# Two of four chunks of the residual x in SBUF, the others in HBM, and the room given to exp outputs and shift buffers

## The chip, the cores and the metric

The kernel runs on one core of a Trainium2 chip. The core has five instruction queues that run beside each other and wait for one another through semaphores: PE (matrix products), ACT (functions such as exp), DVE (vector work), POOL (a second, smaller vector engine) and SP, which here issues the DMAs. Each queue runs its instructions in the order in which they were written down. SBUF is the memory on the core, with 128 partitions; PSUM holds the results of PE in 8 banks; HBM is the large memory, which only DMAs reach. The metric is the device time of one execution in microseconds (us), as the median of several runs.

## The reference

```python
x = A_x                                   # 1 x 2048 x 512, bf16
for layer in range(2):
    # attention, 32 heads of 16
    qkv = layernorm(x) @ wqkv
    p = softmax(q @ k.T * 0.25)           # 2048 x 2048 for each head
    x = x + (p @ v) @ wo
    # dense block
    h = gelu(layernorm(x) @ w1 + b1)      # 2048 x 1792
    x = x + h @ w2 + b2
return x
```

Both layers use the same weights. The norm has no scale or shift of its own.

## The kernel before

**Tiles.** The 2048 tokens are 16 tiles of 128, and four chunks of four tiles. Chunk 0 is tiles 0 to 3, and so on. The residual x lies in SBUF the whole time, as `T["X"]` (L449): 16 tiles of 512 numbers in each partition, 16 KB of bf16 a partition. The attention is worked off in passes (`passes`, L1034): one pass is one chunk of queries, two heads side by side in a tile, and a range of key tiles. Each pass has 64 tiles of scores of 128 x 512 (16 key tiles by four column groups), in sum 4096 over both layers; the first and last passes are cut differently.

**One tile of scores.** PE makes it from `kt` and `qp` (L1168). Its exp is made in one of two ways. On ACT, `exps` (L1503) takes two or three tiles of PSUM at a time (the banks of `SLOTS`, L20) into units of the ring `pt`. On DVE, `dfirst` (L1317) turns one tile from PSUM into 16-bit integers whose bits are nearly the exp, in a buffer of `du`; then `dchain` adds 32 to it (L1378) and 64 to both (L1380), so that four shifted copies stand there. PE multiplies those with V and with three scaled copies of V (`vc`, L1099), and the mean of the four is the better exp. So a DVE tile needs four products where an ACT tile needs one (both L1566, in `pvs`). Only four key tiles of 16 have scaled copies and may go to DVE (`KD`, L45), 512 tiles of scores a layer.

**Buffers.** `pt` has `PT_RING` = 19 units of 1 KB a partition, and borrows parts of K, Q and V when they are not in use (`setup_units`, L1417). `du` has `DU` = 9 tile slots of 4 KB a partition: four pairs, and one half buffer called `dh` (L469 to 473). A pair runs L1378 and L1380 once for two tiles, the half buffer once for one. In layer 1 a fifth pair is borrowed from K of layer 0 (L474, the groups named `kt` in the profile); `cap` (L1083) lists the sizes. A slot is bound when the score's product is issued (`join`, L1207) and free when the last of the four products is issued.

**The order.** Nothing is decided on the chip. When the program is built, `_Sched` (L213) runs the whole computation with costs written beside each operation, and appends each to its engine's list at the time when it would start; semaphore waits follow from what each operation reads and writes (`_Prog`, L81). Threads such as `scores`, `exps`, `pvs` and `post` are Python generators; they yield operations, take units from pools ("acq", "rel") and wait for tokens ("need", "give"). `attach` (L1249), `swap` (L1226) and `solo` (L1325) give a tile to DVE if a slot of `du`, a bank (7, 6, or the third of slot 0) and an eligible tile are to be had and DVE is not behind. `pvs` takes DVE tiles first while more than `PTLOW` = 5 units of `pt` are free, and else ACT tiles (L1550); its products become more urgent with fewer than `PTURG` = 6 free units or with no free `du` buffer (L1542). SP's DMAs are ordered by the same planner, one list for all.

**What uses x.** `loads` (L572) brings it in: chunk 0 in four tiles, chunks 1 to 3 in one DMA each (L578). Three layer norms per chunk follow, which the code calls phases: phase 0 before the projections of layer 0, phase 2 before those of layer 1, phases 1 and 3 before the dense blocks. A norm reads x twice: for statistics on DVE (L612), and for the normalized tile on POOL (L633; on DVE for chunk 0's first one and for the last piece), which a DMA transposes (L637). `wo` adds the attention's output to x (L816), `ytile` the dense block's (L956), both on DVE; in layer 1 `ytile` then writes the tile out (L961). Between these, each chunk of x is not touched for the length of several passes. `post` (L971) runs all of this for a chunk while the passes of the next chunk go on. Weights for it come through a ring of four buffers, one DMA each (`wload`, L858, the DMA in L860).

Of the kernel before, what the change touches and what calls it, by code (L numbers as in the profile page):

```python
# [12 lines left out]
D = 512  # L13
# [7 lines left out]
PVB = 5  # L21
MISC = (6, 7)
DBANK = (7,)
PT_RING = 19
LEND = (3, 2)
QP_RING = 3
W_RING = 4
W_MORE = 4
XLN_RING = 2
GP = 2  # L30

DU = 9
LNP = 7
SWAP = 0.5
ALONE = 3.5
# [392 lines left out]
def bass_interleave_layers__mha_block__dense_activation_gelu__prompt_kernel(  # L428
    nc: bass.Bass,
    A_x: bass.AP,  # L430
    A_wqkv: bass.AP,
    A_wo: bass.AP,
    B_x: bass.AP,
    B_w1: bass.AP,
    B_b1: bass.AP,
    B_w2: bass.AP,
    B_b2: bass.AP,
    out: bass.AP,
):
    S = A_x.shape[1]  # L440
    assert S % 512 == 0 and A_x.shape[2] == D
    NT = S // 128

    with ExitStack() as es:
        def sb(shape, dt, name):
            return es.enter_context(nc.sbuf_tensor(name, shape, dt))

        T = {}
        T["X"] = sb([128, NT, D], BF16, "x")  # L449
        wr = sb([128, W_RING, 1024], BF16, "wr")  # L450
        T["K"] = [sb([128, NDC, S], BF16, "kt%d" % l) for l in range(NL)]
        vf = [sb([128, NT * H * 17], BF16, "v%d" % l) for l in range(NL)]
        T["V"] = [v[:, :].rearrange("p (k h c) -> p k h c", k=NT, h=H) for v in vf]
        T["WR"] = [wr[:, i, :] for i in range(W_RING)]
        T["WR"] += [T["K"][0][:, i // 2, 1024 * (i % 2):1024 * (i % 2) + 1024] for i in range(W_MORE)]
        T["Q"] = sb([128, NDC, S], BF16, "q")
        T["QP"] = sb([128, QP_RING, 512], BF16, "qp")
        T["OTN"] = sb([128, NDC, 512], BF16, "otn")
        T["XF"] = sb([128, NDC, 512], BF16, "xf")
        T["XLN"] = sb([128, XLN_RING, D], BF16, "xln")  # L460
        T["G"] = sb([128, NFC, 512], BF16, "g")
        T["WQKV"] = T["G"][:, 0:12, :].rearrange("p (w c) d -> p w c d", w=3)
        pt = sb([128, PT_RING, 512], BF16, "pt")
# [24 lines left out]
        T["STATS"] = sb([128, NT, 6], F32, "stats")  # L488
        T["MV"] = sb([128, NT, 2], F32, "mv")
        T["VARR"] = sb([128, NT], F32, "varr")  # L490
        T["RSTD"] = sb([128, NT], F32, "rstd")
        T["NMR"] = sb([128, NT], F32, "nmr")
        PS = es.enter_context(nc.psum_tensor("ps", [128, 8 * 512], F32))

        sem_names = ["pe", "act", "dve", "pool", "dxt0", "dxt1", "dxt2", "dxt3", "dx1", "dx2", "dx3", "dwq", "dwk", "dwv", "db1", "db2"] + ["dw%d" % c for c in range(3)] + [
                     "dout"] + ["dwr%d" % i for i in range(W_RING + W_MORE)] + ["dtr%d" % i for i in range(XLN_RING)]
        sems = {n: es.enter_context(nc.semaphore("s_" + n)) for n in sem_names}
        P = _Prog(sems)
        hbm = dict(x=A_x.rearrange("b (n p) d -> p (b n) d", p=128), out=out.rearrange("b (n p) d -> p (b n) d", p=128),
                   wqkv=A_wqkv, wo=A_wo, w1=B_w1, b1=B_b1, w2=B_w2, b2=B_b2)  # L500
        _Plan(P, S, T, PS, hbm).run()

        with nc.Block() as block:
            @block.tensor
            def _(eng):
                P.emit("pe", eng)

            @block.scalar
            def _(eng):
                P.emit("act", eng)  # L510

            @block.vector
# [20 lines left out]
class _Plan:  # L533
# [38 lines left out]
    def loads(self):  # L572
        T, hbm = self.T, self.hbm

        def load(dst, src, sem, keys, cost):
            return _Op("sp", cost, lambda e: e.dma_start(dst, src), writes=keys, sem=sem, by=16, tail=2.0)

        def lx(c):  # L578
            return load(T["X"][:, 4 * c:4 * c + 4, :], hbm["x"][:, 4 * c:4 * c + 4, :], "dx%d" % c,
                        ["X.%d" % t for t in range(4 * c, 4 * c + 4)], 2.5)  # L580

        def lw(i, sem):
            return load(T["WQKV"][:, i, :, :], hbm["wqkv"][:, i * D:(i + 1) * D].rearrange("(c p) f -> p c f", p=128),
                        sem, ["W.%d" % i], 2.5)

        for t in range(4):
            yield load(T["X"][:, t, :], hbm["x"][:, t, :], "dxt%d" % t, ["X.%d" % t], 0.6)
        yield lw(1, "dwk")
        yield lw(0, "dwq")
        yield lw(2, "dwv")  # L590
        yield lx(1)
        yield lx(2)
        yield lx(3)
        yield load(T["B1c"][:], hbm["b1"].rearrange("(c p) -> c p", p=128), "db1", ["B1c"], 0.2)
        yield _Op("sp", 0.2, lambda e: e.dma_start(T["B2row"][0:1, :], hbm["b2"].rearrange("(o e) -> o e", o=1)),
                  reads=["B2zero"], writes=["B2row", "B2zero"], sem="db2", by=16, tail=2.0)
# [5 lines left out]
        yield ("rel", "misc", b)  # L602
        yield ("give", "loaded")

    def ln(self, tiles, dst, dkeys, prio, quick=False):

        T = self.T
# [1 line left out]
        sl = slice(c, c + n)  # L609
        for t in tiles:  # L610
            yield ("need", ("xready", t, self.phase[t // 4]))
            yield _Op("dve", 0.66, lambda e, t=t: e.bn_stats(T["STATS"][:, t, :], T["X"][:, t, :]),  # L612
                      reads=["X.%d" % t], writes=["ST.%d" % t])
            yield _Op("dve", 0.17, lambda e, t=t: e.bn_aggr(T["MV"][:, t, :], T["STATS"][:, t, :]),
                      reads=["ST.%d" % t], writes=["MV.%d" % t])
        mvk = ["MV.%d" % t for t in tiles]
# [11 lines left out]
    def ln_tile(self, c, t, dst, dkeys, quick):  # L628
# [2 lines left out]
        x = yield ("acq", "xln")  # L631
        eng, cost = ("dve", 0.4) if quick else ("pool", 1.0)
        yield _Op(eng, cost, lambda e: e.tensor_scalar(  # L633
            T["XLN"][:, x, :], T["X"][:, t, :], T["RSTD"][:, t:t + 1], T["NMR"][:, t:t + 1], op0=ALU.mult, op1=ALU.add),
            reads=["X.%d" % t, "RSTD.%d" % c, "NMR.%d" % c], writes=["XLN.%d" % x])
        if not quick:
            yield _Op("sp", 0.3, lambda e: e.dma_start(dst(t), T["XLN"][:, x, :], transpose=True),  # L637
                      reads=["XLN.%d" % x], writes=dkeys(t), sem="dtr%d" % x, by=16, tail=3.5)
# [158 lines left out]

    def wo(self, l, seg, t):
        T = self.T
        for gb in range(4):  # L800
            yield ("need", ("otn", l, seg, gb))
        us = []
# [10 lines left out]
                      writes=["B.%d" % b], prio=MID if h else FPRIO, mode="P")  # L813
        for j in range(2):
            yield from self.wdone((l, seg, "O", j), us[j])
        yield _Op("dve", DV, lambda e: e.tensor_tensor(out=T["X"][:, t, :], in0=T["X"][:, t, :], in1=pb, op=ALU.add),  # L816
                  reads=["B.%d" % b, "X.%d" % t], writes=["X.%d" % t])
        yield ("rel", "misc", b)
        yield ("give", ("xready", t, 2 * l + 1))

# [51 lines left out]
    def tiles(self, seg):  # L872
        return range(4 * seg[0] + seg[1] // 128, 4 * seg[0] + (seg[1] + seg[2]) // 128)
# [54 lines left out]
    def ytile(self, l, seg, t):  # L928
# [9 lines left out]
        for p in range(NFC // 2):  # L938
# [14 lines left out]
                      writes=["B.%d" % b], prio=MID if p else FPRIO, mode="P")  # L953
            if not tail or p == last:
                yield from self.wdone(piece, w)
        yield _Op("dve", DV, lambda e: e.tensor_tensor(out=T["X"][:, t, :], in0=T["X"][:, t, :], in1=pb, op=ALU.add),  # L956
                  reads=["B.%d" % b, "X.%d" % t], writes=["X.%d" % t])
        yield ("rel", "misc", b)
        yield ("give", ("xready", t, 2 * l + 2))
        if l == NL - 1:  # L960
            yield _Op("sp", 1.0, lambda e: e.dma_start(self.hbm["out"][:, t, :], T["X"][:, t, :]), reads=["X.%d" % t],  # L961
                      writes=["OUT.%d" % t], sem="dout", by=16, tail=2.0)

    def when(self, l, seg, part):
        return lambda: self.scored >= min(self.base[(l, seg)] + part * self.span[(l, seg)], self.total)
# [56 lines left out]
    def first(self, c):  # L1022
        T = self.T
        self.phase[c] = 0
        for t in range(4 * c, 4 * c + 4):
            yield ("give", ("xready", t, 0))
        tiles = range(4 * c, 4 * c + 4)
        for ts in (tiles,) if c else ([t] for t in tiles):
            yield ("spawn", self.ln(ts, lambda t: T["K"][1][:, :, t * 128:(t + 1) * 128], lambda t: ["XL.%d" % t], 5 + c, c == 0), 5 + c)
# [631 lines left out]
```

## Time and profile before

| what | value |
|---|---|
| median of 3 runs | 1567.77 us (1567.01 to 1567.84) |
| the profiled execution | 1563.99 us |
| its span, first to last instruction | 1562.1 us |
| ACT exps of `pt` (L1503) | 1248 instructions, 1336.7 us |
| scores on PE (L1168) | 4096 products |
| DVE tiles (L1317) into `du`, `dh`, `kt` | 748, 98, 88 |
| first DVE tile, last DVE tile | 65.1 us, 1524.2 us |
| DMA traffic | 96.84 MB |
| weight loads (L860) on SP, B weights | 256 of 256 KB, landing after 2.8 us |

How to read the profile: "busy" is the time in which an engine ran instructions, as a sum and as a share of the span. In a row of a group stand the line, the engine, what is written and read, and the count; behind the bar follow the busy time in us, the mean duration of one in ns, and the idle time just before these with what ended it. In a row of a window stand the window, its length, each engine's busy time and count, the clock granted to PE, the share of DMA and GB/s. In a row of a wait stand who waited for what, the total in us, how often, and the longest. The chain is followed back from the last instruction: at each step to what released it. In a row of DMAs stand the count, the size of one and the median us from issue to landing. The program's span up to some 70 us is the opening (chunk 0 alone, no DVE tiles), 70 to 780 is the rest of layer 0, 780 to 1530 layer 1, and the rest the ending.

### The profile page before, as it was taken

To read this page: it belongs to the slowest core of one execution; us is meant where nothing else is said; L and a number is where in the kernel's file an instruction comes from. 1 tells how busy PE (TensorE), PEld (TensorE's weight loads), DVE (VectorE), ACT (ScalarE), POOL (GpSimd) and SP (SyncE) were. 2 spreads that over 40 slices of the span, in tenths; PEclk is the share of its full clock that TensorE was granted. 3 is DMA by queue.
4 is the path that set the end of the run, shared out by engine and by line. 5 is a ranking of instruction groups with operands and counts; after the bars stand their busy time and mean duration, and the time that the engine had idled before them with its cause. 6 is when DMAs were issued, how large, how long until landed. Compare 5 with 4: busy or idle time off the path is not lost.

```text
span 1562.1 us, 42238 instructions
## 1 busy us (share of the span) xinstructions
PE 1443.7 (92%) x18537; PEld 432.7 (28%) x18537; DVE 1369.9 (88%) x2653; ACT 1523.5 (98%) x1412; POOL 210.5 (13%) x250
## 2 busy tenths in 40 slices
PE   8999889999999999999989999888998989999998
PEld 2222222222222222222222222222222222233344
DVE  5689999979898989978799798999999988898893
ACT  7999999999999999999999999999999999999995
POOL 5300001002020101102030021122002010010000
PEclk9999999999999999999999899999999999999999
DMA  5100001052113310133111331001151105313430
GB/s 143 22 1 1 2 15 35 29 163 55 42 42 116 99 46 26 40 120 102 36 35 42 118 94 42 2 1 35 56 166 52 35 15 161 98 36 96 150 83 29
DMA packets 141765, 96.84 MB, mean 62 GB/s; under 512 B 36877, under 2 KB 141582, under 8 KB 141582
## 3 DMA queue, kind: packets, MB, share of 16 engines
q1 hardware_dynamic: 141582, 94.14, 20.8%
q8 instruction: 146, 2.39, 0.6%
q14 instruction: 37, 0.30, 0.1%
HBM read 84.41 MB, written 2.10 MB: 55 GB/s over the span
## 4 chain that ended last, share of the span: by engine, by line
ACT 65%; PE 24%; DVE 10%; issue 1%; DMA 0%; POOL 0%; ACTq 0%; DVEq 0%
ACT pt L1503 56%; PE ps L543 9%; PE ps L1168 8%; PE ps L1566 6%; DVE du L1317 4%; ACT g L924 3%; ACT kt L1503 2%; ACT v L1503 2%; DVE du L1380 2%; ACT q L1503 1%; DVE du L1378 1%; ACT L924 1%; DVE dh L1317 1%; ACT L1503 0%; PE ps L1156 0%
## 5 line engine op out<-in xcount | busy, mean ns | idle before, releaser
L1503 ACT ACTIVATE pt<-ps 128x1024 bf16<-128x1024 f32 (+1 forms) x1248 | 1336.7, 1232 | 10.7 <-PE ps L1168 8.0
L1168 PE MATMUL ps<-qp,kt 32*128 32x512 bf16 x4096 | 557.8, 386 | 49.7 <-ACT pt L1503 35.0
L1317 DVE TENSOR_SCALAR du<-ps 128x512 uint16<-128x512 f32 x748 | 498.9, 682 | 78.7 <-PE ps L1168 76.3
L1566 PE MATMUL ps<-pt,v 128*17 128x512 bf16 (+1 forms) x3245 | 454.2, 360 | 25.1 <-ACT pt L1503 20.2
L1566 PE MATMUL ps<-du,vc 128*17 128x512 bf16 (+1 forms) x2502 | 353.7, 360 | 8.7 <-ACT pt L1503 5.6
L1168 PEld LDWEIGHTS ps<-qp,kt 32*128 32x128 bf16 x4096 | 143.5, 91 | 611.6 <-ACT pt L1503 409.1
L1380 DVE TENSOR_SCALAR du<-du 128x2048 uint16<-128x2048 uint16 x377 | 257.6, 687 | 2.7
L1116 POOL TENSOR_SCALAR qp<-q,mask 128x512 bf16<-128x512 bf16 (+1 forms) x91 | 80.9, 889 | 958.0 <-PE ps L1168 947.8
L543 PE MATMUL ps<-xf,wr 128*32 128x512 bf16 (+1 forms) x2400 | 168.5, 368 | 1.4 <-DVE g L903 0.7
L1566 PE MATMUL ps<-du,v 128*17 128x512 bf16 (+1 forms) x834 | 160.9, 361 | 6.8 <-DVE v L770 3.1
L1378 DVE TENSOR_SCALAR du<-du 128x1024 uint16<-128x1024 uint16 x377 | 156.4, 424 | 2.5
L1566 PEld LDWEIGHTS ps<-pt,v 128*17 128x17 bf16 x3245 | 111.0, 89 | 138.3 <-issue 64.2
L543 PE MATMUL ps<-wr,g 128*32 128x512 bf16 x1600 | 126.3, 391 | 4.9 <-ACT g L924 4.3
L1566 PEld LDWEIGHTS ps<-du,vc 128*17 128x17 bf16 x2502 | 90.2, 89 | 83.3 <-issue 43.0
L1566 PE MATMUL ps<-dh,vc 128*17 128x512 bf16 (+1 forms) x330 | 95.6, 358 | 0.0
L903 DVE TENSOR_SCALAR g<-ps,hb1t 128x512 bf16<-128x512 f32 (+1 forms) x112 | 79.3, 708 | 5.4 <-PE ps L543 5.0
L1317 DVE TENSOR_SCALAR dh<-ps 128x512 uint16<-128x512 f32 x98 | 66.7, 681 | 1.2 <-PE ps L1168 1.1
L543 PEld LDWEIGHTS ps<-xf,wr 128*32 128x32 bf16 x2400 | 48.1, 95 | 63.0 <-issue 41.0
L1317 DVE TENSOR_SCALAR kt<-ps 128x512 uint16<-128x512 f32 x88 | 60.1, 683 | 5.9 <-PE ps L1168 5.0
L1156 PE MATMUL ps<-vc 128*32 128x512 bf16 x576 | 55.5, 408 | 8.3 <-DVE du L1317 7.3
L633 POOL TENSOR_SCALAR xln<-x,rstd,nmr 128x512 bf16<-128x512 bf16 x58 | 54.3, 939 | 32.9 <-DMA xf<-xln 21.2
L1566 PE MATMUL ps<-kt,vc 128*17 128x512 bf16 (+1 forms) x330 | 57.9, 338 | 0.0
(93 smaller groups left out, 1195.8 us busy)
## 6 DMA issues: line engine op xcount, KB each, us to landing
wr<-in_B_w_dram SPq DMA_DIRECT2D x256, 256.0 KB, 2.8
wr<-in_A_wqkv_dram SPq DMA_DIRECT2D x24, 256.0 KB, 2.8
wr<-in_A_wo_dram SPq DMA_DIRECT2D x18, 256.0 KB, 2.9
out_dram<-x SPq DMA_DIRECT2D x16, 128.0 KB, 2.9
g<-in_A_wqkv_dram SPq DMA_DIRECT2D x3, 512.0 KB, 6.2
x<-in_A_x_dram SPq DMA_DIRECT2D x3, 512.0 KB, 9.1
q<-in_B_w_dram SPq DMA_DIRECT2D x3, 512.0 KB, 5.0
kt<-in_B_w_dram SPq DMA_DIRECT2D x4, 256.0 KB, 3.5
```

Of the source, the lines that this page charges most:

```text
L543: return [lambda e, a=a: e.matmul(out[32 * a:32 * a + 32, :], lhsT=lhsT[:, 32 * a:32 * a + 32], rhs=rhs, start=start, stop=stop, tile_posi ...
L633: yield _Op(eng, cost, lambda e: e.tensor_scalar(T["XLN"][:, x, :], T["X"][:, t, :], T["RSTD"][:, t:t + 1], T["NMR"][:, t:t + 1], op0=ALU. ...
L903: yield _Op("dve", 0.21 + n / 966, lambda e, fc=fc, pb=pb: e.tensor_scalar(T["G"][:, fc, q], pb, T["HB1T"][:, fc:fc + 1], None, op0=ALU.ad ...
L924: lambda e, g=g: e.activation(out=g, in_=g, func=ACT.Gelu_apprx_tanh), reads=gk, writes=gk, prio=2)
L1116: yield _Op("pool", 0.15 + 0.62 * w / 512, lambda e, s=s, q=q, i=i, t=t, w=w: e.tensor_scalar(T["QP"][:, s, w * i:w * i + w], q, T["MASK"] ...
L1156: fns.append(lambda e, o=o, w=w, a=a, m=m: e.matmul(o, lhsT=w, rhs=rhs, start=start, stop=start, tile_position=(0, m * a)))
L1168: return (lambda e: e.matmul(o, lhsT=lhsT, rhs=rhs, start=True, stop=True, tile_position=(32 * a, 0)), ["K%d.%d.%d" % (l, gb, kt // 4), "Q ...
L1317: yield _Op("dve", 0.682, lambda e: e.tensor_scalar(u, self.bank(b), E_SCALE, E_BIAS, op0=ALU.mult, op1=ALU.add), reads=["B.%d" % b], writ ...
L1378: one = _Op("dve", 0.151 + 0.134 * n, lambda e: e.tensor_scalar(U[:, 1, 0:n, :], U[:, 0, 0:n, :], SHIFT, None, op0=ALU.add), reads=key[0], ...
L1380: two = _Op("dve", 0.152 + 0.266 * n, lambda e: e.tensor_scalar(U[:, 2:4, 0:n, :], U[:, 0:2, 0:n, :], 2 * SHIFT, None, op0=ALU.add), reads ...
L1503: yield _Op("act", 0.065 + 0.4267 * n, lambda e, src=src, dst=dst: e.activation(out=dst, in_=src, func=ACT.Exp, scale=0.25), reads=["B.%d" ...
L1566: op.fns.append(lambda e, o=o, lhsT=q[0][0][m], rhs=q[0][1][:, n * m:n * m + n], a=a, st=st, sp=sp: e.matmul(o, lhsT=lhsT, rhs=rhs, start= ...
```

## The change

`X` gets 8 tiles of room instead of 16, and tile t lies at place t modulo 8. So there are two homes: home 0 holds chunk 0 or 2, home 1 chunk 1 or 3. A new thread for each home, `xfeed`, moves chunks in and out by DMAs on SP, through a new HBM tensor `kept`. Its steps for home h:

1. after the phase-0 norm of chunk h: load chunk h + 2 from the input;
2. after the phase-0 norm of chunk h + 2: load chunk h from the input again;
3. after chunk h's norm of phase 2: store it to `kept`, then load chunk h + 2 from the input for its additions in layer 0;
4. after chunk h + 2's norm of phase 2: store it to `kept`, then load chunk h from there;
5. when chunk h is written out in layer 1: load chunk h + 2 from `kept`.

`wo` waits for the chunk (token `xin`). The loads of chunks 2 and 3 that stood in `loads` are gone. The 8 KB of room a partition go to four units of `pt` (19 to 23) and to one more tile slot of `du` (9 to 10); ten slots are five pairs, so there is no half buffer.

```diff
@@ -21,15 +21,16 @@
 PVB = 5
 MISC = (6, 7)
 DBANK = (7,)
-PT_RING = 19
+PT_RING = 23
 LEND = (3, 2)
 QP_RING = 3
 W_RING = 4
 W_MORE = 4
+XT = 8
 XLN_RING = 2
 GP = 2
 
-DU = 9
+DU = 10
 LNP = 7
 SWAP = 0.5
 ALONE = 3.5
@@ -446,7 +447,7 @@
             return es.enter_context(nc.sbuf_tensor(name, shape, dt))
 
         T = {}
-        T["X"] = sb([128, NT, D], BF16, "x")
+        T["X"] = sb([128, XT, D], BF16, "x")
         wr = sb([128, W_RING, 1024], BF16, "wr")
         T["K"] = [sb([128, NDC, S], BF16, "kt%d" % l) for l in range(NL)]
         vf = [sb([128, NT * H * 17], BF16, "v%d" % l) for l in range(NL)]
@@ -493,10 +494,11 @@
         PS = es.enter_context(nc.psum_tensor("ps", [128, 8 * 512], F32))
 
         sem_names = ["pe", "act", "dve", "pool", "dxt0", "dxt1", "dxt2", "dxt3", "dx1", "dx2", "dx3", "dwq", "dwk", "dwv", "db1", "db2"] + ["dw%d" % c for c in range(3)] + [
-                     "dout"] + ["dwr%d" % i for i in range(W_RING + W_MORE)] + ["dtr%d" % i for i in range(XLN_RING)]
+                     "dout", "dk0", "dk1"] + ["dwr%d" % i for i in range(W_RING + W_MORE)] + ["dtr%d" % i for i in range(XLN_RING)]
         sems = {n: es.enter_context(nc.semaphore("s_" + n)) for n in sem_names}
         P = _Prog(sems)
-        hbm = dict(x=A_x.rearrange("b (n p) d -> p (b n) d", p=128), out=out.rearrange("b (n p) d -> p (b n) d", p=128),
+        kept = nc.dram_tensor("kept", [128, NT, D], BF16)
+        hbm = dict(kept=kept[:, :, :], x=A_x.rearrange("b (n p) d -> p (b n) d", p=128), out=out.rearrange("b (n p) d -> p (b n) d", p=128),
                    wqkv=A_wqkv, wo=A_wo, w1=B_w1, b1=B_b1, w2=B_w2, b2=B_b2)
         _Plan(P, S, T, PS, hbm).run()
 
@@ -576,21 +578,24 @@
             return _Op("sp", cost, lambda e: e.dma_start(dst, src), writes=keys, sem=sem, by=16, tail=2.0)
 
         def lx(c):
-            return load(T["X"][:, 4 * c:4 * c + 4, :], hbm["x"][:, 4 * c:4 * c + 4, :], "dx%d" % c,
-                        ["X.%d" % t for t in range(4 * c, 4 * c + 4)], 2.5)
+            return load(T["X"][:, 4 * c % XT:4 * c % XT + 4, :], hbm["x"][:, 4 * c:4 * c + 4, :], "dx%d" % c,
+                        ["X.%d" % (t % XT) for t in range(4 * c, 4 * c + 4)], 2.5)
 
         def lw(i, sem):
             return load(T["WQKV"][:, i, :, :], hbm["wqkv"][:, i * D:(i + 1) * D].rearrange("(c p) f -> p c f", p=128),
                         sem, ["W.%d" % i], 2.5)
 
         for t in range(4):
-            yield load(T["X"][:, t, :], hbm["x"][:, t, :], "dxt%d" % t, ["X.%d" % t], 0.6)
+            yield load(T["X"][:, t % XT, :], hbm["x"][:, t, :], "dxt%d" % t, ["X.%d" % (t % XT)], 0.6)
+            yield ("give", ("xready", t, 0))
         yield lw(1, "dwk")
         yield lw(0, "dwq")
         yield lw(2, "dwv")
         yield lx(1)
-        yield lx(2)
-        yield lx(3)
+        for t in range(4, 8):
+            yield ("give", ("xready", t, 0))
+        yield ("spawn", self.xfeed(0), 3)
+        yield ("spawn", self.xfeed(1), 3)
         yield load(T["B1c"][:], hbm["b1"].rearrange("(c p) -> c p", p=128), "db1", ["B1c"], 0.2)
         yield _Op("sp", 0.2, lambda e: e.dma_start(T["B2row"][0:1, :], hbm["b2"].rearrange("(o e) -> o e", o=1)),
                   reads=["B2zero"], writes=["B2row", "B2zero"], sem="db2", by=16, tail=2.0)
@@ -602,6 +607,44 @@
         yield ("rel", "misc", b)
         yield ("give", "loaded")
 
+    def xmove(self, c, src, dst, sem, reads, writes):
+        yield _Op("sp", 1.5, lambda e: e.dma_start(dst, src), reads=reads, writes=writes, sem=sem, by=16, tail=4.0)
+
+    def xfeed(self, h):
+        keys = ["X.%d" % (t % XT) for t in range(4 * h, 4 * h + 4)]
+        x, kept = self.hbm["x"], self.hbm["kept"]
+        home = self.T["X"][:, 4 * h:4 * h + 4, :]
+        sem = "dx%d" % (h + 2)
+
+        def tiles(c):
+            return range(4 * c, 4 * c + 4)
+
+        def part(src, c):
+            return src[:, 4 * c:4 * c + 4, :]
+
+        for t in tiles(h):
+            yield ("need", ("lnt", t, 0))
+        yield from self.xmove(h, part(x, h + 2), home, sem, [], keys)
+        for t in tiles(h + 2):
+            yield ("give", ("xready", t, 0))
+        for t in tiles(h + 2):
+            yield ("need", ("lnt", t, 0))
+        yield from self.xmove(h, part(x, h), home, sem, [], keys)
+        yield ("give", ("xin", 0, h))
+        for c in (h, h + 2):
+            for t in tiles(c):
+                yield ("need", ("lnt", t, 2))
+            yield from self.xmove(h, home, part(kept, c), "dk%d" % h, keys, ["KEPT.%d" % c])
+            if c == h:
+                yield from self.xmove(h, part(x, h + 2), home, sem, [], keys)
+                yield ("give", ("xin", 0, h + 2))
+        yield from self.xmove(h, part(kept, h), home, sem, ["KEPT.%d" % h], keys)
+        yield ("give", ("xin", 1, h))
+        for t in tiles(h):
+            yield ("need", ("xout", t))
+        yield from self.xmove(h, part(kept, h + 2), home, sem, ["KEPT.%d" % (h + 2)], keys)
+        yield ("give", ("xin", 1, h + 2))
+
     def ln(self, tiles, dst, dkeys, prio, quick=False):
 
         T = self.T
...
@@ -797,6 +840,7 @@
 
     def wo(self, l, seg, t):
         T = self.T
+        yield ("need", ("xin", l, seg[0]))
         for gb in range(4):
             yield ("need", ("otn", l, seg, gb))
         us = []
...
@@ -953,13 +997,14 @@
                       writes=["B.%d" % b], prio=MID if p else FPRIO, mode="P")
             if not tail or p == last:
                 yield from self.wdone(piece, w)
-        yield _Op("dve", DV, lambda e: e.tensor_tensor(out=T["X"][:, t, :], in0=T["X"][:, t, :], in1=pb, op=ALU.add),
-                  reads=["B.%d" % b, "X.%d" % t], writes=["X.%d" % t])
+        yield _Op("dve", DV, lambda e: e.tensor_tensor(out=T["X"][:, t % XT, :], in0=T["X"][:, t % XT, :], in1=pb, op=ALU.add),
+                  reads=["B.%d" % b, "X.%d" % (t % XT)], writes=["X.%d" % (t % XT)])
         yield ("rel", "misc", b)
         yield ("give", ("xready", t, 2 * l + 2))
         if l == NL - 1:
-            yield _Op("sp", 1.0, lambda e: e.dma_start(self.hbm["out"][:, t, :], T["X"][:, t, :]), reads=["X.%d" % t],
+            yield _Op("sp", 1.0, lambda e: e.dma_start(self.hbm["out"][:, t, :], T["X"][:, t % XT, :]), reads=["X.%d" % (t % XT)],
                       writes=["OUT.%d" % t], sem="dout", by=16, tail=2.0)
+            yield ("give", ("xout", t))
 
     def when(self, l, seg, part):
         return lambda: self.scored >= min(self.base[(l, seg)] + part * self.span[(l, seg)], self.total)
@@ -1022,8 +1067,6 @@
     def first(self, c):
         T = self.T
         self.phase[c] = 0
-        for t in range(4 * c, 4 * c + 4):
-            yield ("give", ("xready", t, 0))
         tiles = range(4 * c, 4 * c + 4)
         for ts in (tiles,) if c else ([t] for t in tiles):
             yield ("spawn", self.ln(ts, lambda t: T["K"][1][:, :, t * 128:(t + 1) * 128], lambda t: ["XL.%d" % t], 5 + c, c == 0), 5 + c)
```

Elsewhere each index `t` of X becomes `t % XT` and each key `X.t` becomes `X.(t % XT)`.

More of the change, by code (lines that the diff above doesn't have):

```diff
@@ L611, in ln @@
             yield ("need", ("xready", t, self.phase[t // 4]))
-            yield _Op("dve", 0.66, lambda e, t=t: e.bn_stats(T["STATS"][:, t, :], T["X"][:, t, :]),
-                      reads=["X.%d" % t], writes=["ST.%d" % t])
+            yield _Op("dve", 0.66, lambda e, t=t: e.bn_stats(T["STATS"][:, t, :], T["X"][:, t % XT, :]),
+                      reads=["X.%d" % (t % XT)], writes=["ST.%d" % t])
             yield _Op("dve", 0.17, lambda e, t=t: e.bn_aggr(T["MV"][:, t, :], T["STATS"][:, t, :]),
@@ L633, in ln_tile @@
         yield _Op(eng, cost, lambda e: e.tensor_scalar(
-            T["XLN"][:, x, :], T["X"][:, t, :], T["RSTD"][:, t:t + 1], T["NMR"][:, t:t + 1], op0=ALU.mult, op1=ALU.add),
-            reads=["X.%d" % t, "RSTD.%d" % c, "NMR.%d" % c], writes=["XLN.%d" % x])
+            T["XLN"][:, x, :], T["X"][:, t % XT, :], T["RSTD"][:, t:t + 1], T["NMR"][:, t:t + 1], op0=ALU.mult, op1=ALU.add),
+            reads=["X.%d" % (t % XT), "RSTD.%d" % c, "NMR.%d" % c], writes=["XLN.%d" % x])
         if not quick:
@@ L955, in ytile @@
                 yield from self.wdone(piece, w)
-        yield _Op("dve", DV, lambda e: e.tensor_tensor(out=T["X"][:, t, :], in0=T["X"][:, t, :], in1=pb, op=ALU.add),
-                  reads=["B.%d" % b, "X.%d" % t], writes=["X.%d" % t])
+        yield _Op("dve", DV, lambda e: e.tensor_tensor(out=T["X"][:, t % XT, :], in0=T["X"][:, t % XT, :], in1=pb, op=ALU.add),
+                  reads=["B.%d" % b, "X.%d" % (t % XT)], writes=["X.%d" % (t % XT)])
         yield ("rel", "misc", b)
```

## The prediction

> **What bounds it now.** I read the page first: busy times, then the chain of work that ended last.
>
> ```profile
> span 1562.1 us, 42238 instructions
> ...
> PE 1443.7 (92%) x18537; PEld 432.7 (28%) x18537; DVE 1369.9 (88%) x2653; ACT 1523.5 (98%) x1412; POOL 210.5 (13%) x250
> ...
> ACT 65%; PE 24%; DVE 10%; issue 1%; DMA 0%; POOL 0%; ACTq 0%; DVEq 0%
> ```
>
> ACT is busy for 98% and carries 65% of the chain; DMA carries 0%. So time falls only if ACT gets less to do or waits less. Next, the busy time by stage (PE, PEld, DVE, ACT, POOL), layer 0 and layer 1 without opening and ending:
>
> ```profile
> 70.00:780.00 710.00, 663.45 (x7895) 181.93 (x7887) 635.85 (x1218) 702.68 (x650) 85.11 (x89) 1.00 0.19 53
> 780.00:1530.00 750.00, 691.17 (x9307) 214.74 (x9300) 685.95 (x1326) 744.17 (x682) 91.62 (x106) 0.99 0.24 69
> ```
>
> ACT idles 7.3 + 5.8 = 13.1 us in these 1460 us, DVE 74.2 + 64.1 = 138.3, PE 46.6 + 58.8 = 105.4. There are 4096 tiles of scores (L1168 x4096 on the page); each gets its exp on ACT (L1503) or on DVE (L1317, then L1378 and L1380). A DVE tile is thus a tile that ACT is spared. The same two stages for L1317 alone (DVE busy and count):
>
> ```profile
> 70.00:780.00 710.00, 296.69 (x446) 1.00 0.19 53
> 780.00:1530.00 750.00, 322.32 (x486) 0.99 0.24 69
> ```
>
> 446 / 710 = 0.628 DVE tiles per us with nine tile slots in DU, and 486 / 750 = 0.648 with eleven (layer 1 has the borrowed pair). Four key tiles of 16 may go to DVE, 512 tiles a layer; with two before 70 us, 64 are left over in layer 0 and 26 in layer 1. What ACT waits for at its exps, from the waits (total, times, longest):
>
> ```profile
> ACT pt L1503 <- PE ps L1168: 8.0, 12, 2.1
> ACT pt L1503 <- PE ps L1566: 2.0, 2, 1.7
> ACT v L1503 <- PE ps L1566: 1.0, 3, 0.4
> ```
>
> Only the last two, 3.0 us, are waits for a free exp output.
>
> **An ACT tile's price.** In the timeline, exps that follow each other begin 0.904 us apart with two tiles and 1.330 with three: 0.426 per tile, 0.052 per instruction. **A DVE tile's price** stands in the DVE groups by shape (busy, mean ns):
>
> ```profile
> L1317 DVE TENSOR_SCALAR du<-ps 128x512 uint16<-128x512 f32 x748 | 498.9, 682 | 78.7 <-PE ps L1168 76.3
> L1380 DVE TENSOR_SCALAR du<-du 128x2048 uint16<-128x2048 uint16 x371 | 255.3, 692 | 2.7
> L1378 DVE TENSOR_SCALAR du<-du 128x1024 uint16<-128x1024 uint16 x371 | 154.8, 426 | 2.5
> L1317 DVE TENSOR_SCALAR dh<-ps 128x512 uint16<-128x512 f32 x98 | 66.7, 681 | 1.2 <-PE ps L1168 1.1
> L1380 DVE TENSOR_SCALAR dh<-dh 128x1024 uint16<-128x1024 uint16 x98 | 41.1, 420 | 0.7
> L1378 DVE TENSOR_SCALAR dh<-dh 128x512 uint16<-128x512 uint16 x98 | 29.2, 298 | 0.5
> ```
>
> In a pair: 0.682 + (0.692 + 0.426) / 2 = 1.241 us. Alone in the half buffer `dh`: 0.681 + 0.420 + 0.298 = 1.399.
>
> **The change, part by part.**
>
> (1) *One more tile slot* (DU 9 to 10; ten slots in layer 0, twelve in layer 1). Upper bound: slots alone set the rate, so it grows by 1/9 and 1/11: +50 tiles, and +44 of which 26 are to be had; 76 tiles, 32.4 us of ACT. Lower bound: no tile, 0; the gain below zero is a rival. Nearest row: two slots more went with 0.020 per us more, 0.010 a slot; over 710 and 750 us that is 7 + 7 = 14 tiles, **6.0 us**. I take this, since it is the same resource in the same kernel, although layer 1 has other DVE work beside it. 14 tiles cost DVE 17.4 us of its 138 idle.
>
> (2) *The half buffer becomes a pair.* 98 tiles x 0.158 = 15.5 us less DVE work. If DVE time were the limit this were 12 more tiles, 5.3 us; if not, 0. DVE waits 76.3 us for scores at L1317 alone, so time is mostly not its limit: a quarter, 3 tiles, **1.3 us**.
>
> (3) *Four more exp outputs.* At most the 3.0 us above; 1.7 of it is one wait near 90 us, where PE is the busy engine (19.7 of the 20 us from 60 on). I take a third, **1.0 us**.
>
> [...]
>
> (4) *PE.* A DVE tile has four products where an ACT tile has one (four shifted copies), four columns at a time every 0.22 us in the timeline: 3 x 0.22 / 4 = 0.165 us more. For 17 tiles 2.8 us, beside 105 us of idle PE: 0 here, 2.8 without that cover.
>
> (5) *Moving x.* Seven moves of 512 KB a home where there was one: 14 instead of 2, so 12 more on SP's queue, 6.3 MB on 96.84. Rows for such moves:
>
> ```profile
> out_dram<-x SPq DMA_DIRECT2D x16, 128.0 KB, 2.9
> ...
> x<-in_A_x_dram SPq DMA_DIRECT2D x3, 512.0 KB, 9.1
> q<-in_B_w_dram SPq DMA_DIRECT2D x3, 512.0 KB, 5.0
> ...
> x<-in_A_x_dram SPq DMA_DIRECT2D x4, 128.0 KB, 2.3
> ```
>
> A load lands in 5.0 to 9.1 us; a store to HBM between 2.9 (a quarter of the size) and, doubled for caution, 18.2. Store and load in a row: 8 to 27 us. Now the slack, from the starts in the timeline. Chunk 0's last read by the layer norm of phase 2 is at 373.6 and chunk 2's first add at 597.8; chunk 1's at 548.8, chunk 3's add at 785.6. Back again: chunk 2 read by 739.1, chunk 0's add at 1048.9; chunk 3 read by 931.7, chunk 1's add at 1177.7. In the last layer: chunk 0 written out at 1175.7, chunk 2's add at 1351.4; chunk 1 at 1335.8, chunk 3's add at 1474.7. The least is 139 us. All adds are covered: **0**; without cover each late load would stop DVE's adds for 5 to 9 us.
>
> On SP's queue the load that follows a store in the same home waits for the store, and weight loads (L860) stand behind it. Who waited for L860 in the whole run: PE, 1.0 us in five times. The stores come after the norms (374, 551, 740, 933), where the next weights are 8 us or more off. 0 taken; at the extreme four stores of 18.2 with nothing between, 73 us, which needs every weight load to be needed at once, so I keep only some 8 us of it for the range.
>
> [...] No run here yet shows an SP store of 512 KB.
>
> (6) *The opening.* Chunk 2's load waits for chunk 0's norm (last read at 8.2 us instead of a free issue at 5); its statistics began at 17.7, and fewer transfers share the queue: 0. Chunk 3's load waits for chunk 1's norm on POOL, whose last read ends at 27.0, and for its transposes (last issued 27.5): it lands at 32.5 to 36.6, plus four statistics (4 x 0.83) and a power of 1.3, so 37 to 41. Its first normalization on POOL was at 45.7 and its first key projection came out at 79.1. But the statistics are on DVE's in-order queue, before value copies (L714, L765) that PE waits for; a load later than planned holds them, by up to 9.1 - 5.0 = 4.1 us. I take **+1.0** (0 to 4.1).
>
> Sum: -6.0 - 1.3 - 1.0 + 1.0 = **-7.3 us**. The profiled execution took 1563.99 (span 1562.1 and 1.9 around it), so 1556.7; the median of the runs is 1567.77, 3.8 above it: **1560.5**. Measurement tells changes of some 0.2%, 3.1 us, from none.
>
> **Rivals.**
>
> *A, slots are the limit alone.* All 76 tiles: -32 us, 1535. For it: counted from the timeline (L1317's starts less the ends of the last products), 5.9 tiles are in flight on the mean in layer 0 but nine at times. Against: 0.648 after two more slots is far from 0.628 x 11 / 9 = 0.768. 0.06.
>
> *B, new slots stay empty.* DVE tiles also need a bank, 7 or 6 or one of slot 0's three; 82.4 us of DVE's idle before L1317 end with PE's scores. If banks or PE's order decide, only (2), (3) and (6) are left: -1 to +1, 1567. 0.18.
>
> *C, slower: products lag and hold the slots.* `pvs` serves DVE tiles first while more than five exp outputs are free (L1550) and hurries while fewer than six are (L1542). With 23 outputs it hurries less, PE's products fall behind the scores, and each DU slot is held longer. Nine slots at 0.628 per us give 14.3 us a tile; ten break even at 15.9, twelve in layer 1 at 18.5 (17.0 now). Beyond that, DVE's share falls. Price: the lowest stage, 1400 to 1530, has 78 tiles in 130 us, 0.600 against 932 / 1460 = 0.638; at that rate 56 tiles go back to ACT, +24 us; half of it, +12 us: 1580. For it: the new order is written once for all, ACT's idle of 0.9% in the middle leaves little to win and much to lose. Against: ACT waits only 3.0 us for outputs, so the ring is rarely near empty. 0.31.
>
> **Numbers.** Forecast (1550 to 1564) 0.45, A 0.06, B 0.18, C 0.31. Faster 0.45 + 0.06 = 0.51, same 0.18, slower 0.31. Low 1550: the forecast with 12 tiles more; high 1583: C with some late weights. That leaves out A and about a third of C, some 0.15. The forecast's own range is 1550 to 1564.
>
> **What would show it.** L1317 in sum about 951 instead of 934, ACT's exp tiles 17 fewer, no `dh`; adds L816 with no wait for DMA; L860 still hardly waited for. Wrong, if L1317's count is at or under 934, if ACT idles over 20 us between 70 and 1530, or if DVE waits for x's DMAs before 60 us by over 4.

## The result, and the profile after

The changed kernel's median is 1558.54 us (1557.2 to 1565.0, eight runs) against 1568.57 us (1567.0 to 1573.8) of before: ratio 0.9939, interval 0.9921 to 0.9957, about 9.6 us faster. The forecast was 1560.5, 7.3 us faster. The size held; the largest term of its sum did not, so that the agreement is luck, as the step-by-step part shows.

First the changed kernel's page, the same parts as were shown of before:

```profile
span 1560.9 us, 42388 instructions
...
PE 1442.4 (92%) x18658; PEld 431.4 (28%) x18658; DVE 1368.6 (88%) x2561; ACT 1524.0 (98%) x1407; POOL 204.1 (13%) x250
...
ACT 67%; PE 22%; DVE 10%; issue 1%; DMA 0%; POOL 0%; SPq 0%; ACTq 0%
```

ACT has as much to do as before (1523.5). The two stages (PE, PEld, DVE, ACT, POOL), then the same two for the DVE tiles alone (the line is L1360 now):

```profile
70.00:780.00 710.00, 663.32 (x7959) 181.40 (x7953) 638.76 (x1177) 704.78 (x653) 87.12 (x95) 1.00 0.20 58
780.00:1530.00 750.00, 689.66 (x9367) 215.03 (x9362) 680.14 (x1274) 741.91 (x674) 83.35 (x101) 0.99 0.25 71
```

```profile
70.00:780.00 710.00, 299.14 (x451) 1.00 0.20 58
780.00:1530.00 750.00, 320.35 (x481) 0.99 0.25 71
```

There are five DVE tiles more in layer 0 and five fewer in layer 1 (one, begun just before 780 us, counts in both windows); by the groups below there are 855 + 79 = 934 in all, as before. ACT idles 5.2 + 8.1 = 13.3 us in the middle, before 13.1. So neither less work for ACT nor less waiting in the middle explains 9.6 us. The profiled executions themselves hardly differ: 1562.71 us after and 1563.99 before, at the same granted clock (0.992). The difference lies in what the other executions do. Here are the span and the mean granted clock of one execution each of the kernel before, the one shown first, and of the same kernel run again:

```profile
core 0: 1562.1 us, clock 0.992
```

```profile
core 0: 1570.4 us, clock 0.986
```

The same program took 8.3 us more at a clock lower by 0.006. Over 87 executions of before that were recorded beside the experiments, a straight line through time against clock gives 1557.4 us at full clock, and 0.99 us more for each 0.001 that the clock is lower. Single executions scatter about this line by 0.85 us; of the 8.3 us above it gives some 6. Before's mean clock is 0.989, the changed kernel's 0.995.

What the clock does shows in single windows of the kernel before. In both pairs, ACT's two long gelus begin in the first window or shortly before:

```profile
864.60:868.20 3.60, 1.42 (x21) 0.44 (x17) 3.53 (x7) 3.59 (x3) 0.00 (x0) 1.00 0.05 15
868.20:871.60 3.40, 3.40 (x26) 0.65 (x18) 1.18 (x3) 3.38 (x2) 0.00 (x0) 0.50 0.28 82
...
1270.90:1274.40 3.50, 1.12 (x24) 0.54 (x28) 3.50 (x8) 3.50 (x2) 2.28 (x1) 1.00 0.01 2
1274.40:1277.80 3.40, 3.40 (x36) 1.13 (x28) 0.79 (x2) 3.37 (x3) 0.00 (x0) 0.50 0.00 0
```

PE is busy 1.42 of 3.60 us in the first window, 1.12 of 3.50 in the third; in the 3.4 us after each the clock (third number from the end) is 0.50. PE's longest wait in the first window, then in the third:

```profile
PE ps L543 <- ACT g L924: 1.9, 1, 1.9
```

```profile
PE ps L1156 <- DVE du L1317: 3.0, 1, 3.0
```

In one it waits for the gelu's result itself, in the other, by the profile, for a DVE tile. PE was not always as idle as that: before another low stretch it was busy for 2.35 of 3.40 us.

```profile
919.40:922.80 3.40, 2.35 (x26) 0.68 (x24) 3.40 (x8) 3.40 (x4) 0.00 (x0) 1.00 0.00 0
922.80:926.20 3.40, 3.38 (x26) 0.63 (x25) 2.57 (x8) 3.10 (x4) 1.81 (x2) 0.50 0.00 0
```

The low stretches in the trace of before are four of 3.41 us and one of 10.24; in that of the change three of 3.41 and two of 6.83, and one that begins 0.2 us before the span ends. One window of 3.41 us at 0.50 is 1.7 us of lost clock, 0.0011 of the span, and so, at 0.99 us for 0.001, about 1.1 us of time. Before's 0.0108 of lost clock is some ten windows an execution, the changed kernel's 0.0050 between four and five.

### The profile page after: what moved, and what is told of

Its sections match the earlier page's. It is cut to its first block, busy times and chain, and to the rows that moved or that the text cites. A ratio compares the mean times of both kernels' runs of the same rounds, so it can differ in the third digit from the quotient of the medians.

```text
span 1560.9 us, 42388 instructions
## 1 busy us (share of the span) xinstructions
PE 1442.4 (92%) x18658; PEld 431.4 (28%) x18658; DVE 1368.6 (88%) x2561; ACT 1524.0 (98%) x1407; POOL 204.1 (13%) x250
## 4 chain that ended last, share of the span: by engine, by line
ACT 67%; PE 22%; DVE 10%; issue 1%; DMA 0%; POOL 0%; SPq 0%; ACTq 0%
ACT pt L1546 59%; PE ps L545 8%; PE ps L1211 7%; PE ps L1609 7%; DVE du L1360 4%; ACT g L968 3%; DVE du L1423 2%; ACT v L1546 2%; ACT kt L1546 1%; DVE du L1421 1%; ACT q L1546 1%; ACT L1546 1%; ACT L968 1%; DVE kt L1360 0%; DVE x L860 0%
## 5 line engine op out<-in xcount | busy, mean ns | idle before, releaser
L1546 ACT ACTIVATE pt<-ps 128x1024 bf16<-128x1024 f32 (+1 forms) x1280 | 1372.9, 1235 | 11.8 <-PE ps L1211 9.5
L1360 DVE TENSOR_SCALAR du<-ps 128x512 uint16<-128x512 f32 x855 | 569.4, 682 | 85.3 <-PE ps L1211 82.6
L1609 PE MATMUL ps<-pt,v 128*17 128x512 bf16 (+1 forms) x3346 | 441.4, 361 | 20.9 <-ACT pt L1546 17.3
L1609 PE MATMUL ps<-du,vc 128*17 128x512 bf16 (+1 forms) x2868 | 373.8, 360 | 10.0 <-ACT pt L1546 5.9
L1423 DVE TENSOR_SCALAR du<-du 128x2048 uint16<-128x2048 uint16 (+1 forms) x432 | 295.9, 690 | 3.4
L1159 POOL TENSOR_SCALAR qp<-q,mask 128x512 bf16<-128x512 bf16 (+1 forms) x91 | 70.4, 774 | 968.1 <-PE ps L1211 957.9
L1609 PE MATMUL ps<-du,v 128*17 128x512 bf16 (+1 forms) x956 | 170.9, 362 | 11.1 <-ACT pt L1546 7.2
L1421 DVE TENSOR_SCALAR du<-du 128x1024 uint16<-128x1024 uint16 (+1 forms) x432 | 178.4, 426 | 3.1
L828 POOL TENSOR_TENSOR ott<-xt,rc 128x256 bf16<-128x256 f32 x42 | 32.2, 766 | 207.2 <-DVE rc L820 178.4
L1609 PEld LDWEIGHTS ps<-du,v 128*17 128x17 bf16 x956 | 43.9, 88 | 55.2 <-issue 16.0
L1360 DVE TENSOR_SCALAR kt<-ps 128x512 uint16<-128x512 f32 x79 | 53.8, 681 | 2.6 <-PE ps L1211 2.3
```

The lines of the kernel that those rows point to most:

```text
L1159: yield _Op("pool", 0.15 + 0.62 * w / 512, lambda e, s=s, q=q, i=i, t=t, w=w: e.tensor_scalar(T["QP"][:, s, w * i:w * i + w], q, T["MASK"] ...
L1360: yield _Op("dve", 0.682, lambda e: e.tensor_scalar(u, self.bank(b), E_SCALE, E_BIAS, op0=ALU.mult, op1=ALU.add), reads=["B.%d" % b], writ ...
L1421: one = _Op("dve", 0.151 + 0.134 * n, lambda e: e.tensor_scalar(U[:, 1, 0:n, :], U[:, 0, 0:n, :], SHIFT, None, op0=ALU.add), reads=key[0], ...
L1423: two = _Op("dve", 0.152 + 0.266 * n, lambda e: e.tensor_scalar(U[:, 2:4, 0:n, :], U[:, 0:2, 0:n, :], 2 * SHIFT, None, op0=ALU.add), reads ...
L1546: yield _Op("act", 0.065 + 0.4267 * n, lambda e, src=src, dst=dst: e.activation(out=dst, in_=src, func=ACT.Exp, scale=0.25), reads=["B.%d" ...
L1609: op.fns.append(lambda e, o=o, lhsT=q[0][0][m], rhs=q[0][1][:, n * m:n * m + n], a=a, st=st, sp=sp: e.matmul(o, lhsT=lhsT, rhs=rhs, start= ...
```

## The experiments

Theories: **S**, the new slot gives ACT's work to DVE (the forecast's main term); **R**, the exp outputs; **X**, moving x; **G**, the room as a whole; **L** (also called P below), the planner's list order, which any edit throws anew; **K**, the clock. "At full clock" is the mean time less 1.0 us per 0.001 of mean clock missing, the slope of before; lines through the other kernels' own runs give 0.7 to 1.1.

| kernel | room (exp outputs, slots) | DVE tiles | median us | ratio to before, interval | mean clock | at full clock |
|---|---|---|---|---|---|---|
| before, 87 runs | 19, 9 | 934 | 1568 | | 0.989 | 1557.3 |
| before_again | 19, 9 | 934 | 1567.4 | 1.0000 (0.9985 to 1.0015) | 0.989 | 1557.0 |
| before_tol | 19, 9 | 928 | 1564.9 | 0.9981 (0.9967 to 0.9995) | 0.994 | 1558.9 |
| before_lat | 19, 9 | 924 | 1570.8 | 1.0022 (1.0008 to 1.0036) | 0.993 | 1564.9 |
| before_warm | 19, 9 | 934 | 1565.4 | 0.9978 (0.9966 to 0.9990) | 0.993 | 1558.3 |
| x_only | 19, 9, x moves | 925 | 1568.9 | 1.0008 (0.9993 to 1.0022) | 0.995 | 1563.5 |
| x_ring | 23, 9, x moves | 929 | 1564.4 | 0.9985 (0.9969 to 1.0001) | 0.996 | 1560.7 |
| x_slot | 19, 10, x moves | 933 | 1566.6 | 0.9999 (0.9985 to 1.0012) | 0.994 | 1561.1 |
| the change | 23, 10 | 934 | 1558.5 | 0.9939 (0.9921 to 0.9957) | 0.995 | 1554.7 |
| after_tol | 23, 10 | 929 | 1562.4 | 0.9966 (0.9954 to 0.9978) | 0.995 | 1557.1 |
| after_lat | 23, 10 | 939 | 1567.3 | 1.0000 (0.9987 to 1.0012) | 0.994 | 1561.2 |
| after_lat22 | 23, 10 | 939 | 1554.2 | 0.9911 (0.9893 to 0.9928) | 0.997 | 1550.7 |
| after_warm | 23, 10 | 934 | 1557.8 | 0.9935 (0.9917 to 0.9953) | 0.997 | 1555.5 |
| two_halves | 23, 10 (4 pairs, 2 halves) | 937 | 1555.1 | 0.9919 (0.9900 to 0.9939) | 0.995 | 1550.6 |

x_only and before_tol do not give the reference's result: their output is off by 0.24 (relative error), and why is not known. Their times are shown as those of an order of the work, and what rests on them is also given without them.

### The parts one by one

**x_only**: the changed kernel with the old room.

```diff
-PT_RING = 23
+PT_RING = 19
-DU = 10
+DU = 9
```

> The changed kernel with 19 exp outputs and nine DU slots: x moves through HBM, the freed room stays unused. Its program gives DVE 925 tiles of scores, 9 fewer than before's 934. Theory S (slots: the gain comes from the new DU slot) and theory R (the gain comes from the four exp outputs): the gain is gone, ratio to before 1.000 to 1.004 (9 tiles back on ACT at 0.426 are 3.8 us, 0.24%). Theory X (moving x early shortens the opening or frees DVE): ratio about 0.994 as in the changed kernel. Theory P (the two hand-outs of work differ by the luck of one list order, whatever the room): anything from 0.994 to 1.006, not ordered with the room.

**x_ring**:

```diff
-DU = 10
+DU = 9
```

> x moves, 23 exp outputs, nine DU slots (half buffer kept); 929 DVE tiles. Theory R: the gain stays, ratio about 0.994. Theory S: ratio about 1.000 (5 tiles fewer than before, +2.1 us, 1.001). Theory X: 0.994. Theory P: 0.994 to 1.006.

**x_slot**:

```diff
-PT_RING = 23
+PT_RING = 19
```

> x moves, 19 exp outputs, ten DU slots as five pairs; 933 DVE tiles. Theory S: the gain stays, about 0.994 to 0.996. Theory R: ratio about 1.000. Theory X: 0.994. Theory P: 0.994 to 1.006. If S and R each hold in part, both single kernels lie between 0.994 and 1.000.

Measured 1.0008, 0.9985, 0.9999. X gets no support: with the moves alone nothing is gained in this order. Neither S nor R alone gives 0.994. At full clock all three are slower than before, by 3 to 6 us, and their clock is higher, by 5 to 7 us worth: two things move in each of these kernels, and so the three by themselves settle nothing between "both are needed" and L. Among the kernels that move x, at full clock, the slot takes 2.4 us off x_only with 8 tiles more, the exp outputs 2.8 us with 4, both together 8.8 us with 9. This is one order each, and the next experiments show how little one order says.

**before_again**: no edit.

> The kernel before, unchanged, to see the span and the granted clock of each of its runs. The profiled execution shown before took 1563.99 us, under all eight runs of it (1567.0 to 1573.8), while the changed kernel's profiled execution (1562.71) lies within its runs (1557.2 to 1565.0). If the clock explains the 9.6 us, before's runs show a lower granted clock (under 0.99) than the changed kernel's (0.990 to 0.997) and runs of one clock differ by about 1 us. If not, before's runs show 0.99 or more and take about 1568 all the same. Ratio 1.000.

Clocks of 0.986 to 0.995 came with 1572.2 to 1562.6 us. The profiled execution shown before was one of the better ones at 0.992; that is why it lies under the runs it was shown with. Time goes with the clock within one and the same program: a line through these twelve runs gives 0.96 us for 0.001. Which of the two makes the other these runs do not tell; before_warm below does.

### The same room in another order

**before_tol** and **before_lat** change the kernel before, **after_tol**, **after_lat** and **after_lat22** the changed one, each in one figure that the planner calculates with and that the chip never sees.

```diff
-TOL = 0.2
+TOL = 0.19
```

(0.21 in after_tol)

```diff
-LATENCY = {"pe": 0.219, "act": 0.21, "dve": 0.139, "pool": 0.153328, "sp": 0.1}
+LATENCY = {"pe": 0.218, "act": 0.21, "dve": 0.139, "pool": 0.153328, "sp": 0.1}
```

(0.22 in after_lat22)

> The kernel before with one constant of its planner changed that belongs to no resource (TOL 0.2 to 0.19: how late a bank may come free and still take a DVE tile). The program orders its work anew; 928 DVE tiles. Theory G (the room itself pays, about 8 us): stays at before's time, within 3 us of 1567.8. Theory L (the time at one clock is the luck of one list order): anywhere within 8 us of it, as far as the room seemed to pay. Read at full clock (the fit of time against granted clock, 1 us for 0.001), before has 1557.3, the changed kernel 1554.7.

> The kernel before with the planner's figure for PE's signal 0.218 instead of 0.219; 924 DVE tiles. Theory G: within 3 us of 1567.8. Theory L: anywhere within 8 us; 10 DVE tiles fewer alone would be +4.3 us.

> The changed kernel with TOL 0.21; 929 DVE tiles. Theory G: stays ahead of before, about 1558 to 1562, ratio 0.994 to 0.996. Theory L: anywhere from 1555 to 1568, no closer to the changed kernel than to before.

> The changed kernel with PE's signal at 0.218; 939 DVE tiles. Theory G: ratio 0.992 to 0.996. Theory L: anywhere from 1555 to 1568. If the number of DVE tiles decides, it is 2 us ahead of the changed kernel.

> The changed kernel with the planner's figure for PE's signal 0.220 instead of 0.219, one more order of the same work with the same room; 939 DVE tiles. Theory L: 1555 to 1568, with the three orders of the changed kernel so far at 1558.5, 1562.4 and 1567.3. Theory G: under 1564. If the number of DVE tiles decides: 5 tiles x 0.426 = 2.1 us under the changed kernel, 1556.4.

Measured: 1564.9 and 1570.8 with the old room, 1562.4, 1567.3 and 1554.2 with the new. L holds: the order alone is worth 6 us among three orders with the old room (3 among two without before_tol) and 13 among four with the new, and after_lat is no faster than before. G's stronger form falls with that. A weaker one stays possible: at full clock the four kernels with the old room (before, before_tol, before_lat, and x_only, which also moves x) are at 1561.2 on the mean with a scatter of 3.6, the four orders with the new room at 1555.9 with 4.4. The difference is 5.2 us, with an uncertainty of 2.9 (the root of a quarter of the sum of their squares), which is under two uncertainties and so not shown. Without x_only and before_tol two old orders are left, 1557.3 and 1564.9: the same difference, with an uncertainty of 4.4. The number of DVE tiles goes the same way, 927.8 and 935.3 on the mean: 7.5 tiles with an uncertainty of 3.3, or 3.2 us at 0.426. But it doesn't decide alone: after_lat and after_lat22 both have 939 and lie 10.5 us apart at full clock.

### The clock

**before_warm** and **after_warm**: the planner puts in more filler products, which compute nothing that is used and only keep PE active.

```diff
-WARM = 0.38
+WARM = 0.45
```

> The kernel before with more filler products on PE (WARM 0.38 to 0.45: idle PE time is filled while the planned activity of the last 2.5 us is below this). The order of DVE, ACT, POOL and SP is the same as in the kernel before, instruction for instruction; only filler products are added on PE. In the runs so far one half-clock window of 3.41 us costs about 1.1 us (1.0 to 1.1 us for 0.001 of mean clock); before's mean clock is 0.990, the changed kernel's 0.995. Theory K (over half of the 9 us is the clock): the mean clock rises to about 0.995 and the time falls by about 5 us, to 1562 to 1563, ratio about 0.9965; read at full clock it stays at 1557. Rival: the clock has nothing to do with it, or the fillers take PE time that the products need: time at 1568 or above.

> The changed kernel with WARM 0.45, again only filler products added on PE. Theory K: mean clock from 0.995 to 0.997 or more, time down by 1 to 3 us, 1556 to 1558, ratio 0.992 to 0.993; at full clock still 1554.7. Rival: PE has no room left for fillers, 1559 or above.

The main filler group in the kernel before, and in before_warm:

```profile
L1156 PE MATMUL ps<-vc x576: 376/389/635, 32.2 to 1545.8; 128*32 128x512 bf16 x192
```

```profile
L1156 PE MATMUL ps<-vc x860: 376/389/634, 32.3 to 1546.2; 128*32 128x512 bf16 x172
```

284 products more of this kind, with the four other queues in the same order, raised the mean clock from 0.989 to 0.993. By means the time fell from 1568.2 to 1565.4 us: 3.7 us by the clock at the slope of before, less 1.0 us lost at full clock; that the fillers stand in PE's way there is argued, not shown. So K holds as a cause, with 2.8 of the 3.7 us arriving, though these fillers closed less than I expected (0.995). In after_warm the clock rose by 0.002 and its mean time fell by 1.5 us.

### Pair or two halves

**two_halves**: ten slots as four pairs and two half buffers.

```diff
-        du = sb([128, DU // 2, 4, 2, 512], U16, "du")
-        T["DU"] = [du[:, i, :, :, :] for i in range(DU // 2)]
-        if DU % 2:
-            half = sb([128, 4, 1, 512], U16, "dh")
-            T["DU"].append(half[:, :, :, :])
+        du = sb([128, DU // 2 - 1, 4, 2, 512], U16, "du")
+        T["DU"] = [du[:, i, :, :, :] for i in range(DU // 2 - 1)]
+        half = sb([128, 2, 4, 1, 512], U16, "dh")
+        T["DU"] += [half[:, i, :, :, :] for i in range(2)]
...
-        self.cap = [2] * (DU // 2) + [1] * (DU % 2) + [2]
+        self.cap = [2] * (DU // 2 - 1) + [1, 1] + [2]
```

> The changed kernel with its ten DU slots as four pairs and two half buffers, instead of five pairs; 937 DVE tiles. Theory pair (step 2 of the forecast: the pair's cheaper DVE work matters): twice 98 or so tiles cost 0.158 us more each on DVE, up to 31 us of DVE work; as DVE idles over 130 us, at most 25 us x 0.34 of ACT, so 1558 to 1567. Theory slot: the same as the changed kernel, 1558.5 within 2. Theory L (list order): anywhere within 8 us, 1555 to 1568.

Its DVE groups of the half buffers:

```profile
L1359 DVE TENSOR_SCALAR dh<-ps 128x512 uint16<-128x512 f32 x179 | 121.6, 681 | 6.3 <-PE ps L1210 5.8
L1422 DVE TENSOR_SCALAR dh<-dh 128x1024 uint16<-128x1024 uint16 x179 | 75.3, 423 | 1.1
L1420 DVE TENSOR_SCALAR dh<-dh 128x512 uint16<-128x512 uint16 x179 | 52.5, 300 | 0.7
```

Its busy times:

```profile
PE 1440.1 (93%) x18702; PEld 432.5 (28%) x18702; DVE 1380.0 (89%) x2740; ACT 1520.8 (98%) x1401; POOL 202.2 (13%) x250
```

There are 179 tiles at the dearer price, some 28 us more DVE work than with pairs by the mean durations. DVE's busy time is only 11.4 us above the change's (1368.6), since the durations of DVE's instructions overlap in the trace: its groups add up to 1550.1 us. The kernel is faster than the change all the same (1555.1), with 937 DVE tiles for 934. That speaks against DVE's time as the limit of the number of tiles; with one order, and five tiles of scatter between orders, it doesn't decide about so few as the 3 of the forecast. That this arrangement beats five pairs isn't shown: the lead over the change is within what another order makes.

after_lat22 and two_halves beat both kernels, by 0.89% and 0.81% against before.

## Why the forecast came out right, step by step

(1) *The slot* failed as the prediction put it, and with it the largest term, 6.0 of 7.3 us: 14 tiles more, of 17 in sum, were forecast, and DVE got none. The prediction's own sign of being wrong, a count at or under 934, came true. Its row (nine slots against eleven in one kernel) set a rate against a rate where other work also differed. Over four orders each the room goes with 7.5 tiles, less than half of the 17. Before's own order had the most tiles of its four, 934 against 924 to 928, which may have hidden them.

(2) *The pair*: the cheaper instructions came, the tiles did not. The three groups that replace those of the half buffer, for du, with no `dh` left:

```profile
L1360 DVE TENSOR_SCALAR du<-ps 128x512 uint16<-128x512 f32 x855 | 569.4, 682 | 85.3 <-PE ps L1211 82.6
...
L1423 DVE TENSOR_SCALAR du<-du 128x2048 uint16<-128x2048 uint16 x423 | 291.8, 694 | 3.4
L1421 DVE TENSOR_SCALAR du<-du 128x1024 uint16<-128x1024 uint16 x423 | 176.2, 429 | 3.1
```

Over all three buffers the durations of a tile's three operations add up to 1142.3 us, 17.6 less than before. But DVE's busy time on the page fell only from 1369.9 to 1368.6 us: the groups of before add up to 1528.5 us, so durations overlap, and the difference of two prices taken from mean durations, 1.399 less 1.241, was more than DVE was spared here. DVE's idle time before L1360 is 85.3 us for `du`, before 78.7; that says nothing, for the kernel before itself, run again, has

```profile
L1317 DVE TENSOR_SCALAR du<-ps 128x512 uint16<-128x512 f32 x748 | 498.8, 682 | 84.8 <-PE ps L1168 82.5
```

Forecast 1.3 us; no run shows it, and two_halves speaks against it.

(3) *The exp outputs*: forecast 1.0; the waits for a free output fell by 1.5. ACT's waits at the exps, then one of the kernel before, run again:

```profile
ACT pt L1546 <- PE ps L1211: 9.5, 16, 1.2
...
ACT pt L1546 <- PE ps L1609: 1.5, 3, 1.0
```

```profile
ACT pt L1503 <- PE ps L1168: 14.5, 24, 1.9
```

Waits for a free output fell from 3.0 to 1.5. Those for scores rose from 8.0 to 9.5, so that in this pair of executions nothing is left of it in the sum; but they differ by more than that between two executions of before, 8.0 and 14.5, so that the worth of the four outputs stays open.

(4) *PE* was not tested, as no DVE tiles were added: 663.3 and 689.7 us busy in the stages against 663.5 and 691.2.

(5) *Moving x* cost nothing on the path, as forecast. The moves, with the median from issue to landing, and SP's wait for its stores:

```profile
x<-in_A_x_dram SPq DMA_DIRECT2D x7, 512.0 KB, 4.4
kept<-x SPq DMA_DIRECT2D x4, 512.0 KB, 2.9
x<-kept SPq DMA_DIRECT2D x4, 512.0 KB, 3.9
```

```profile
SPq L611 <- DMA kept<-x: 9.4, 4, 2.4
```

A 512 KB store lands in 2.9 us, at the lower end of my bounds. A store of a quarter of the size took as long (2.9 before, 2.8 now). SP stood 9.4 us in four waits, and PE waited 2.6 us for weights in the whole run (before 1.0). The additions waited for no DMA:

```profile
L860 DVE TENSOR_TENSOR x<-x,ps x32: 673/678/689, 217.4 to 1538.5; 128x512 bf16<-128x512 bf16 x32
its engine sat idle before it (us, times) until:
  PE ps L545: 6.0, 7
```

(6) *The opening*: forecast +1.0, measured +0.3 (ACT busy 61.7 of the first 70 us, before 62.0). DVE waited 1.1 us for x at its first statistics, before 1.2; the late load of chunk 3 stopped nobody.

*What stands in place of (1).* By means the runs differ by 1568.2 - 1559.7 = 8.5 us (before as the mean of the 87 executions, whose clocks are on record). The clock gives 0.995 - 0.989, 5.8 us. The prediction had no term for it, though the page's row of the clock had nines and one eight. It put the median 3.8 us above the profiled execution, as before; the changed kernel's median lies 4.2 us below its own, and the two profiled executions differ by 1.3 us where 7.3 were forecast. So the number came out by the clock, by luck. Of the other 2.6 us at full clock, most may lie in the ending; ACT's waits from 1525 us on, before and after:

```profile
ACT xf L650 <- PE ps L644: 7.7, 1, 7.7
...
ACT g L898 <- PE ps L543: 3.5, 2, 2.6
```

```profile
ACT g L942 <- PE ps L545: 4.8, 2, 2.6
ACT xf L693 <- PE ps L687: 4.2, 1, 4.2
```

11.2 us became 9.0 (before_again has the same 11.2). The order can move this too, with either room. Here are before_tol, with the old room, and after_lat, with the new:

```profile
ACT xf L650 <- PE ps L644: 4.4, 1, 4.4
```

```profile
ACT xf L693 <- PE ps L687: 7.7, 1, 7.7
```

before_lat, with the old room, has 4.0 at that wait and is the slowest kernel at full clock, so the ending is only a part of what an order changes.

*The range.* The low end is said to be the forecast with 12 tiles more; 12 x 0.426 is 5.1 us, which gives 1555 and not 1550.

*Rivals.* A is out. B was right about the tiles of this pair and wrong about the time. C's mechanism did not come: the tile rate is 451 / 710 = 0.635 and 481 / 750 = 0.641, near before's 0.628 and 0.648, and the waits for outputs fell. Its argument, that a new order can lose, was sound: after_lat shows it.

What stays open: how much of the 2.6 us at full clock is the room's own, and whether the room lifts the clock. The four old-room kernels have 0.989, 0.994, 0.993, 0.995, the four new ones 0.995, 0.995, 0.994, 0.997; without the kernel before there is little between them. I take before's low clock for the luck of its order; this is argued, not shown.

## What to carry to other kernels

Where a program is laid out by a planner, run a few orders that differ in a figure without meaning before the effect of one edit is believed; here such orders spread by 6 to 13 us, and the edit's effect was 9.6. Read the granted clock beside each time and split the difference into clock and work, since a profile of one execution can hide either: here the two profiled executions differ by 1.3 us, the means by 8.5. Cheaper work on an engine that is not the limit need not show in the time: count what the bound engine is spared, here the tiles, and read the freed engine's busy time as a whole, since durations can overlap; here DVE's three operations for a tile fell by 17.6 us in sum and its busy time by 1.3.

## What the runs showed of the hardware that was not expected

By the slope of 0.99 us for 0.001 of clock, a window of 3.41 us at 0.50 costs about 1.1 us in a kernel whose PE is busy for 92% but whose ACT is busy for 98%: less than the 1.7 us of clock that it takes, more than nothing. And the clock varies from run to run of one program: over the 87 executions of before it goes from 0.982 to 0.995 and the time from 1562.7 to 1574.7 us, with an identical instruction list.
